# Turning q and k by squares of 32 from the sixteenth pair of heads, and natural token order from the third batch

## The chip, the cores and the metric

The kernel runs on one core of a Trainium2 chip. A core has TensorE (PE in the profile) for matrix products, VectorE (DVE), ScalarE (ACT) and GpSimd (POOL) for elementwise work, and SyncE (SP), whose queue issues nearly all of this kernel's DMA transfers. Each engine has its own list of instructions; semaphores order them against each other. The metric is the time of one execution on the device in microseconds (us); less is better.

## What is computed

Attention with normed queries and keys, then a two-layer network with the activation h - tanh(h):

```python
# q, k, v: (8 batches, 12 heads, 448 tokens, 64); g_q, g_k: (64,)
def rmsnorm(x, g):
    rms = np.sqrt(np.mean(x * x, axis=-1, keepdims=True) + 1e-06)
    return x / rms * g
q_n, k_n = rmsnorm(q, g_q), rmsnorm(k, g_k)
scores = 1.0 / np.sqrt(64) * np.matmul(q_n, k_n.transpose(0, 1, 3, 2))
attn = np.exp(scores - np.max(scores, axis=-1, keepdims=True))
attn = attn / (np.sum(attn, axis=-1, keepdims=True) + 1e-09)
o = np.matmul(attn, v)
x = o.transpose(0, 2, 1, 3).reshape(8 * 448, 12 * 64)
h = x @ w_in                       # w_in: (768, 2048)
out = (h - np.tanh(h)) @ w_out     # w_out: (2048, 768)
```

All data are float32, the weights float64 in memory.

## The kernel before, in words

Heads are taken two at a time, so there are 8 x 6 = 48 pairs, numbered s = 0 to 47; six pairs make a batch. The program is written out by hand, slot by slot: one slot of the schedule per pair (the functions `first_slot`, `early_slot` and `slot`). What stands in a slot for pair s is mixed with preparations for the pairs s + 1 to s + 4. Between these pieces, `run(gap)` draws as many matrix products of the network's stream (`mlp`, a generator) as fit a budget of time; the stream is one batch behind attention. In a slot from 12 on there are eight such runs, and each batch's stream fills six slots: three with the first layer (`hidden`), three with the second (`project`).

*The stream.* Both layers use a scheme of seven products in place of eight (`products`, line 712; the products are the matmuls of L733). A product's weights come from a ring of six slots in SBUF that SP fills from scratch memory (`ring_load`, L386 and L388), five products ahead. Each product is added into s1, s2 or s5 on DVE or ACT as soon as it is done (L787 to L803), and three PSUM banks take turns, with products 2, 3 and 7 accumulating on top of 1, 5 and 6. In the first batch the weights are still being made: each 768 KB piece of float64 words is fetched (`w_raw`, L265 and L269), rounded in three stages on ACT (L71, L72), DVE (L78 to L82) and POOL (L90), with three buffers for the raw words. That ends in slot 10; the first batch's second layer (`project_first`, L898) runs in slots 9 to 11.

*The old way of q and k.* `load` (through `fetch`) brings q and k of pair s + 4 in slot s. `squares` takes their squares on ACT (L123, L124), `norm` sums and scales on DVE and raises to the power -1/2 on POOL (L133 to L135), both for pair s + 3; `norm_q` scales q (L410 on DVE, or L408 on ACT for pairs 9 to 14); and `turn` transposes k and q of pair s + 2 on PE, four transposes each (L421, L425), with evictions from PSUM on ACT (L423, L429). The scale of k is applied later, as the per-partition scale of the exponentials (L512).

*By squares of 32.* From batch `FIRST` on, here 3, `by_blocks(s)` is true. `load_blocks` (L447) fetches q and k of pair s + 3 by eight DMAs in 32 x 32 squares of tokens and dimensions; `square_blocks` (L451, ACT), `norm_blocks` (L458 to L463, DVE and one power on POOL), `scale_blocks` (L470, DVE) and `turn_blocks` (L480 and L484, DVE transposes within the squares, L485 on ACT) follow in the next slot, for pair s + 2. Nothing of it is on PE. It needs the pool `late["blocks"]`, opened when `project_first` has ended.

*Order of tokens.* In the first three batches a partition of the q, k and v tiles holds neighbouring tokens (q four of them, k and v three), so that a piece of memory is 1 KB for q and 768 B for v. Squares of 32 keep tokens in natural order, and from batch 3 on v is fetched in natural order too (`fetch(..., in_order)`), in pieces of 256 B; the last 64 tokens of k and v are always apart (L118). `store` (L828) turns a result back and undoes the permuted order for batches below `FIRST`.

*Attention.* `visit` (for pairs from 13) interleaves the products p x v of pair s (L567, L555) with the scores of pair s + 1 (L506); exponentials are on ACT (L512). The sums of the exponentials are folded on DVE (L537 to L545, L640, L642) and spread (L650 to L663).

Queues are strictly what the program order makes them: SP's list holds, in a slot from 12 on, the ring loads of its runs, the loads of v, and the loads of q and k in their places.

Of the kernel before, what the change touches and what calls it, by code (L numbers as in the profile page):

```python
# [20 lines left out]
NCH = 4  # L21
# [71 lines left out]
def fetch(nc, name, t, pair, in_order=False):  # L93

    S = pair.shape[1]
    P = 128
    KF, KR = S // P, S % P
    if name == "q":
        nc.sync.dma_start(
            out=t.rearrange("p h c d -> p h (c d)"), in_=pair.rearrange("h (p c) d -> p h (c d)", c=NCH)  # L100
        )
        return
    full, rest = pair[:, : KF * P].rearrange("h (p c) d -> h p c d", c=KF), pair[:, KF * P :]
    if name == "v":
        last = t[:, :, KF]
    if in_order:
        for h in range(2):
            nc.sync.dma_start(out=t[:, h, :KF], in_=pair[h, : KF * P].rearrange("(c p) d -> p c d", p=P))
    elif name == "v":
        nc.sync.dma_start(  # L110
            out=t[:, :, :KF].rearrange("p h c d -> p h (c d)"), in_=full.rearrange("h p c d -> p h (c d)")
        )
    else:
        last = t[:, KF]
        for h in range(2):
            nc.sync.dma_start(out=t[:, :KF, h], in_=full[h])
    for r in range(2):
        nc.sync.dma_start(out=last[r * KR : (r + 1) * KR], in_=rest.rearrange("h p d -> p h d"))  # L118
# [19 lines left out]
def bounded_path(tc, ctx, q, k, v, moe_w_in, moe_w_out, out, g_col, ident, ones, half_ones, neg_half, early):  # L138
# [17 lines left out]
    nc = tc.nc  # L156
    B, H, S, D = q.shape
    DFF, DM = moe_w_out.shape
    P = 128
    CP = S // NCH  # L160
    NP = H // 2
# [12 lines left out]
    BL = 32  # L174
    KF, KR = S // P, S % P
# [32 lines left out]
    def load(s, names):  # L208
        b, hp = steps[s]
        for name in names:  # L210
            src = {"q": q, "k": k, "v": v}[name]
            if s == 0 and name != "v":
                t = early[name]
            else:
                shape = [CP, 2, NCH, D] if name == "q" else [P, NCH, 2, D] if name == "k" else [P, 2, NCH, D]
                t = nat.tile(shape, F32, name=f"{name}_nat", bufs=3 if name == "v" else 2)
                fetch(nc, name, t, src[b, 2 * hp : 2 * hp + 2], by_blocks(s))
            loaded[name, s] = t


# [172 lines left out]
    def squares(s):  # L393
        squares_of(nc, early["sq"], early["n"], loaded["q", s], loaded["k", s])
# [36 lines left out]

    FIRST, NJ = 3, S // BL

    def by_blocks(s):
        return has(s) and steps[s][0] >= FIRST

    def load_blocks(s):
        b, hp = steps[s]  # L440
        t = loaded["qk", s] = late["blocks"].tile([P, 2, NJ, BL], F32, name="qk_nat", bufs=2)
        for i, src in enumerate((q, k)):
            for h in range(2):
                rows = src[b, 2 * hp + h].rearrange("(j t) (m d) -> m t j d", t=BL, d=BL)
                for m in range(2):
                    r = (2 * h + m) * BL
                    nc.sync.dma_start(out=t[r : r + BL, i], in_=rows[m])  # L447
# [27 lines left out]
    def turn_blocks(s, i):  # L475

        n = normed[s][:, i].rearrange("p j d -> p (j d)")
        if i == 0:
            qT = qkp.tile([P, S], F32, name="qT")
            nc.vector.transpose(out=qT, in_=n)  # L480
            turned[s] = qT
            return
        kT = qkp.tile([P, S], F32, name="kT")
        nc.vector.transpose(out=kT, in_=n)  # L484
        nc.scalar.mul(kT, kT, g_col)  # L485
        turned[s] = None, kT, turned[s]
        del normed[s]

    def sc_bank():
        return bank_of("sc")  # L490
# [38 lines left out]
    def add(s):  # L529

        if s <= NP + NP // 2:
            sums[s] = []
            return
        t = early["sum"]
        sums[s] = [t]
        p = full(s)
        nc.vector.tensor_tensor(out=t, in0=p[0], in1=p[1], op=ALU.add)  # L537
        nc.vector.tensor_tensor(out=t, in0=t, in1=p[2], op=ALU.add)
# [72 lines left out]
    def totals(s, dn):  # L611

        parts = [t[:, h, n * HS : (n + 1) * HS] for t in sums.get(s, ()) for n in range(2) for h in range(2)]
        parts = [(parts, [ones[:, :BL]] * 2)] if parts else []
        if not sums.pop(s):
            for p in full(s):
                parts.append(
                    ([p[:, h, n * HS : (n + 1) * HS] for n in range(2) for h in range(2)], [ones[:, :BL]] * 2)
                )
            last = probs[s, KF]  # L620
            parts.append(([last[:, h, 0] for _ in range(2) for h in range(2)], [half_ones[:, n] for n in range(2)]))
        for i, (moving, by) in enumerate(parts):
            for n in range(2):
                for h in range(2):
                    r = (2 * n + h) * BL
                    nc.tensor.matmul(
                        dn[r : r + BL, :HS], lhsT=by[n], rhs=moving[2 * n + h],
                        start=(i == 0), stop=(i == len(parts) - 1),
                    )
        rs = whole[s] = sp.tile([P, HS], F32, name="rs")  # L630
        nc.vector.reciprocal(rs, dn[:, :HS])  # L631
# [290 lines left out]
    def run(ns):  # L922

        spent[1] += ns
        while spent[0] + 1.0 < spent[1]:
            took = next(stream, None)
            if took is None:
                return
            spent[0] += took
# [4 lines left out]
    def gap_ns(s):  # L934

        if s < 2 * NP:
            return H_NS / 12 if s % NP < 3 else 4 * S / ENGINE_NS * CD * CF / 12
        return (H_NS + O_NS) / (4 * NP)

    def has(s):  # L940
        return 0 <= s < NS

    def first_slot(s):
# [6 lines left out]
        if s > -3:  # L950
            load(s + 4, "qk")
# [5 lines left out]
        if has(s + 2):  # L957
            load(s + 2, "v")
# [18 lines left out]
    def early_slot(s):  # L977
        gap = gap_ns(s)
        totals(s, sc_bank())
        if has(s + 1):  # L980
            scores(s + 1, 0)
            scores(s + 1, 1)
        if has(s + 2):
            load(s + 2, "v")
        run(gap)
        if has(s + 2):
            turn(s + 2, sc_bank(), sc_bank())
        if has(s + 3):
            squares(s + 3)
        if has(s + 4):  # L990
            load(s + 4, "qk")
        run(gap)
        if has(s + 1):
            scores(s + 1, KF)
        av = [sc_bank() for _ in range(2)]
        last_values(s, av)
        divide(s, values(s, av))
        if has(s + 1):
            scores(s + 1, 2)
        for work, n in ((add, 1), (add_last, 1), (norm, 3), (norm_q, 3)):  # L1000
            run(gap / 2)
            if has(s + n):
                work(s + n)

    def slot(s):

        gap = gap_ns(s)
        av = av_banks
        if has(s + 1):
            scores(s + 1, KF)  # L1010
        if s < FOLDED:
            last_values(s, av)
            totals(s, sc_bank())
            divide(s, values(s, av))
            for c in range(KF):
                scores(s + 1, c)
        else:
            visit(s, av)
        if has(s + 2):
            load(s + 2, "v")  # L1020
        if by_blocks(s + 3):
            load_blocks(s + 3)
        blocks = by_blocks(s + 2)
        run(gap / 2)
        if has(s + 1):
            add(s + 1)
        if blocks:
            square_blocks(s + 2)
        run(gap / 2)
        if blocks:  # L1030
            norm_blocks(s + 2)
        elif has(s + 2):
            turn(s + 2, sc_bank(), sc_bank())
        ahead = has(s + 3) and not by_blocks(s + 3)
        if ahead:
            squares(s + 3)
        if has(s + 4) and not by_blocks(s + 4):
            load(s + 4, "qk")
        run(gap / 2)
        folded = has(s + 1) and s + 1 >= FOLDED  # L1040
        if has(s + 1):
            add_last(s + 1)
        if folded:
            fold(s + 1)
        run(gap / 2)
        if blocks:
            scale_blocks(s + 2)
        if ahead:
            norm(s + 3)
        if folded:  # L1050
            gather(s + 1, 0)
        run(gap / 2)
        if blocks:
            turn_blocks(s + 2, 0)
        if folded:
            gather(s + 1, 1)
        run(gap / 2)
        if blocks:
            turn_blocks(s + 2, 1)
        if ahead:  # L1060
            norm_q(s + 3)
        run(gap / 2)
        if folded:
            spread_sums(s + 1)
        run(gap / 2)
# [358 lines left out]
```

## Time and profile before

| what | value |
|---|---|
| median of 3 runs | 1404.11 us (1401.81 to 1405.44) |
| the profiled execution's own time | 1404.34 us |
| its span, first to last instruction | 1402.5 us |
| PE busy, slots of the early part, 206.8 to 240.5 us | 31.70 of 33.70 us |
| PE busy, slots 13 to 15 (323.1 to 407.0 us) | all of it |
| DMA queue of SP | 355120 packets, 248.00 MB, 64.7% of 16 engines' span |
| weight fetches w_raw, second layer | 16 of 768 KB, 5.4 us to landing |
| fetches of q, whole, in the old way | 17 of 224 KB, 4.8 us to landing |
| fetches of q in squares | 120 of 56 KB, 2.4 us to landing |

The profile is of one execution. Times are counted from the first instruction. A row of the groups names a line of the kernel, the engine, the operation, what it writes and reads, its count, then the busy time in us, the mean of one in ns, and the idle time of the engine just before, with what ended it. The chain of work is followed back from the last instruction to what released each step. PE's matmuls are pipelined, so busy times of short runs overlap.

### The profile page before, as it was taken

To read this page: it belongs to the slowest core of one execution; us is meant where nothing else is said; L and a number is where in the kernel's file an instruction comes from. 1 tells how busy PE (TensorE), PEld (TensorE's weight loads), DVE (VectorE), ACT (ScalarE), POOL (GpSimd) and SP (SyncE) were. 2 spreads that over 40 slices of the span, in tenths; PEclk is the share of its full clock that TensorE was granted. 3 is DMA by queue.
4 is the path that set the end of the run, shared out by engine and by line. 5 is a ranking of instruction groups with operands and counts; after the bars stand their busy time and mean duration, and the time that the engine had idled before them with its cause. 6 is when DMAs were issued, how large, how long until landed. Compare 5 with 4: busy or idle time off the path is not lost.

```text
span 1402.5 us, 29929 instructions
## 1 busy us (share of the span) xinstructions
PE 1367.2 (97%) x11864; PEld 1135.0 (81%) x11864; DVE 939.3 (67%) x1530; ACT 506.6 (36%) x1153; POOL 556.4 (40%) x348
## 2 busy tenths in 40 slices
PE   6999899999999999999999999999999999999997
PEld 2458664478888888888889988988988998899997
DVE  3999888866756688567867668656885678632311
ACT  5866554234422433233332333224333243301100
POOL 4665555223532246225544246422462254411310
PEclk9999999999999999999999999999999999999999
DMA  7769788864556656666666666666666666366563
GB/s 174 178 187 252 241 253 212 223 188 153 172 150 179 175 167 172 173 152 200 173 153 173 188 159 180 181 158 175 168 165 175 164 183 186 109 188 179 191 193 91
DMA packets 355273, 250.01 MB, mean 178 GB/s; under 512 B 266484, under 2 KB 297396, under 8 KB 355124
## 3 DMA queue, kind: packets, MB, share of 16 engines
q1 hardware_dynamic: 355120, 248.00, 64.7%
q8 instruction: 96, 1.57, 0.5%
q14 instruction: 53, 0.43, 0.1%
q10 hardware_dynamic: 4, 0.00, 0.0%
HBM read 214.50 MB, written 33.42 MB: 177 GB/s over the span
## 4 chain that ended last, share of the span: by engine, by line
PE 87%; DVE 5%; DMA 3%; ACT 2%; SPq 2%; issue 1%; POOL 0%; DVEq 0%; ACTq 0%
PE mm L733 64%; PE sc L506 9%; PE sc L567 6%; PE mm L898 4%; PE sc L555 1%; PE sc L605 1%; DMA w_raw<-in_moe_w_out_dram 1%; DMA gT<-in_moe_w_in_dram 1%; DMA q_nat<-in_q_dram 1%; ACT p L512 1%; SPq L118 1%; PE mm L605 1%; DMA w_f<-w_out 0%; DVE rs L631 0%; DVE w_out L82 0%
## 5 line engine op out<-in xcount | busy, mean ns | idle before, releaser
L733 PE MATMUL mm<-xT,w_f 128*128 128x224 f32 x1392 | 278.2, 354 | 2.3 <-DVE s L789 2.3
L733 PEld LDWEIGHTS mm<-xT,w_f 128*128 128x128 f32 x1392 | 261.3, 190 | 15.9 <-issue 10.2
L733 PEld LDWEIGHTS mm<-gT,w_f 128*128 128x128 f32 x1344 | 252.8, 190 | 13.2 <-issue 13.2
L733 PE MATMUL mm<-gT,w_f 128*128 128x224 f32 x1344 | 263.0, 354 | 0.0
L506 PE MATMUL sc<-qT,kT 64*32 64x448 f32 (+1 forms) x3072 | 219.3, 507 | 11.7 <-ACT p_last L512 7.8
L463 POOL TENSOR_TENSOR rr_mine<-rr_mine,neg_half 128x28 f32<-128x28 f32 x30 | 145.1, 4837 | 205.5 <-DVE rr_mine L462 205.5
L733 PE MATMUL mm<-tt,w_f 128*128 128x224 f32 x1044 | 208.9, 353 | 0.0
L733 PEld LDWEIGHTS mm<-tt,w_f 128*128 128x128 f32 x1044 | 196.6, 190 | 4.8 <-issue 4.4
L733 PE MATMUL mm<-tg,w_f 128*128 128x224 f32 x1008 | 197.7, 352 | 0.0
L770 POOL TENSOR_TENSOR gT<-s,th 128x448 f32<-128x448 f32 x96 | 119.1, 1250 | 189.4 <-ACT th L769 184.5
L733 PEld LDWEIGHTS mm<-tg,w_f 128*128 128x128 f32 x1008 | 190.6, 190 | 0.0
L506 PEld LDWEIGHTS sc<-qT,kT 64*32 64x32 f32 x3072 | 75.3, 106 | 87.7 <-issue 52.9
L671 DVE TENSOR_TENSOR xT<-xT,sc 128x448 f32<-128x448 f32 x35 | 21.7, 621 | 175.5 <-ACT xT L670 146.9
L693 POOL TENSOR_TENSOR tt<-xT,tt 128x224 f32<-128x224 f32 x23 | 31.4, 1367 | 243.6 <-DVE xT L675 222.0
L650 ACT COPY sum_g<-sum 32x14 f32<-32x14 f32 x280 | 56.2, 201 | 183.7 <-DVE sum L642 178.0
L567 PE MATMUL sc<-p,v_nat 64*32 64x448 f32 x1120 | 110.5, 536 | 0.0
L769 ACT ACTIVATE th<-s 128x448 f32<-128x448 f32 x96 | 55.2, 575 | 116.4 <-DVE s L795 57.2
L512 ACT ACTIVATE p<-sc 128x448 f32<-128x448 f32 x120 | 65.3, 544 | 58.0 <-PE sc L506 34.5
L135 POOL TENSOR_TENSOR rr<-rr,neg_half 112x8 f32<-112x8 f32 (+1 forms) x36 | 59.6, 1678 | 61.8 <-DVE rr L134 37.8
L898 PE MATMUL mm<-gT,w_out 128*128 128x448 f32 x192 | 75.5, 548 | 0.2 <-POOL w_out L90 0.2
L898 PEld LDWEIGHTS mm<-gT,w_out 128*128 128x128 f32 x192 | 36.1, 192 | 38.5 <-issue 36.4
L567 PEld LDWEIGHTS sc<-p,v_nat 64*32 64x32 f32 x1120 | 42.0, 107 | 30.6 <-issue 30.6
(151 smaller groups left out, 1853.7 us busy)
## 6 DMA issues: line engine op xcount, KB each, us to landing
w_f<-w_in SPq DMA_DIRECT2D x196, 384.0 KB, 3.3
w_f<-w_out SPq DMA_DIRECT2D x147, 512.0 KB, 4.0
w_raw<-in_moe_w_out_dram SPq DMA_DIRECT2D x16, 768.0 KB, 5.4
out_dram<-th SPq DMA_DIRECT2D x192, 56.0 KB, 1.9
w_in<-w_out SPq DMA_DIRECT2D x21, 384.0 KB, 6.5
qk_nat<-in_q_dram SPq DMA_DIRECT2D x120, 56.0 KB, 2.4
qk_nat<-in_k_dram SPq DMA_DIRECT2D x120, 56.0 KB, 2.4
gT<-in_moe_w_in_dram SPq DMA_DIRECT2D x32, 192.0 KB, 4.2
```

The lines of the kernel that those rows point to most:

```text
L135: nc.gpsimd.tensor_tensor(out=r, in0=r, in1=neg_half[:rows], op=ALU.pow)
L463: nc.gpsimd.tensor_tensor(out=mine, in0=mine, in1=neg_half[:, :1].to_broadcast([P, 2 * NJ]), op=ALU.pow)
L506: nc.tensor.matmul(tiles[h][i * BL : (i + 1) * BL, :n], lhsT=kT[r, c * P + at : c * P + at + BL], rhs=qT[r, first : first + n], start=True ...
L512: nc.scalar.activation(p[:, h, c if c < 2 else 0, :], tiles[h][:, :n], AF.Exp, scale=1.0 if rr is None else rr[:, 0, 2 * c + h : 2 * c + h ...
L567: nc.tensor.matmul(av[g][i * BL : (i + 1) * BL, :S], lhsT=v_nat[keys, h, c, m * BL : (m + 1) * BL], rhs=p[keys, h], start=first, stop=True ...
L605: nc.tensor.matmul(av[n][r : r + BL, :HS], lhsT=v_nat[:, h, c, m * BL : (m + 1) * BL], rhs=p[c][:, h, n * HS : (n + 1) * HS], start=False, ...
L650: nc.scalar.copy(out=acc[h * BL : (h + 1) * BL, g], in_=part[g * BL : (g + 1) * BL, h * NJ : (h + 1) * NJ])
L693: eng.tensor_tensor(out=t2, in0=x22, in1=t1, op=ALU.subtract)
L733: nc.tensor.matmul(bank[:, f * HS : (f + 1) * HS], lhsT=w[:, c * width + f, :], rhs=moving[p](c), start=(first and f == 0 and c == 0), sto ...
L769: nc.scalar.activation(th, h, AF.Tanh, bias=0.0, scale=1.0)
L770: eng.tensor_tensor(out=g[:, rows, cols], in0=h, in1=th, op=ALU.subtract)
L898: nc.tensor.matmul(bank[:, :S], lhsT=w_out_row(f, n // HC)[:, n % HC * P : (n % HC + 1) * P], rhs=g[:, f, :], start=(f == 0), stop=(f == C ...
```

## The change

Squares of 32 now begin with pair `TURNED` = 2 x 6 + 3 = 15, in the middle of the third batch (numbered 2), instead of pair 18. Since squares keep the natural order and a batch must have one order, `FIRST` becomes 2: all of the third batch is fetched in natural order. Its first three pairs (12, 13, 14) still go the old way, so `fetch` learns to bring q and k in natural order, in pieces of 256 B: q by two DMAs instead of one. v of pairs 12 to 17 is fetched like that of later batches, by two DMAs for the full part instead of one. The store of the third batch needs no reordering. The fetches of q and k of pairs 15 to 17 in the old way leave slots 11 to 13. The first fetch of squares, of pair 15, stands near the end of slot 12 rather than behind the load of v, since the pool of the squares is opened only within that slot; those of pairs 16 and 17 stand in slots 13 and 14 at the usual place.

```diff
@@ fetch
     if name == "q":
+        if in_order:
+            for h in range(2):
+                nc.sync.dma_start(out=t[:, h], in_=pair[h].rearrange("(c p) d -> p c d", c=NCH))
+            return
         nc.sync.dma_start(
...
     if name == "v":
         last = t[:, :, KF]
+    elif in_order:
+        last = t[:, KF]
     if in_order:
         for h in range(2):
-            nc.sync.dma_start(out=t[:, h, :KF], in_=pair[h, : KF * P].rearrange("(c p) d -> p c d", p=P))
+            to = t[:, h, :KF] if name == "v" else t[:, :KF, h]
+            nc.sync.dma_start(out=to, in_=pair[h, : KF * P].rearrange("(c p) d -> p c d", p=P))
@@ load
-                fetch(nc, name, t, src[b, 2 * hp : 2 * hp + 2], by_blocks(s))
+                fetch(nc, name, t, src[b, 2 * hp : 2 * hp + 2], in_order(s))
@@
-    FIRST, NJ = 3, S // BL
+    FIRST, NJ = 2, S // BL
+    TURNED = 2 * NP + 3
 
     def by_blocks(s):
+        return has(s) and s >= TURNED
+
+    def in_order(s):
         return has(s) and steps[s][0] >= FIRST
@@ early_slot
-        if has(s + 4):
+        if has(s + 4) and not by_blocks(s + 4):
             load(s + 4, "qk")
@@ slot
-        if by_blocks(s + 3):
+        if by_blocks(s + 3) and s + 3 > TURNED:
             load_blocks(s + 3)
...
         if blocks:
             turn_blocks(s + 2, 1)
+        if s + 3 == TURNED:
+            load_blocks(s + 3)
         if ahead:
             norm_q(s + 3)
```

## The prediction

> **What bounds the kernel now.** I read the page's busy row first, then the chain of work that ended last in order of time, then the groups of instructions, the waits, and the timelines of SP, DVE, ACT and POOL around two places. The busy row:
>
> ```profile
> PE 1367.2 (97%) x11864; PEld 1135.0 (81%) x11864; DVE 939.3 (67%) x1530; ACT 506.6 (36%) x1153; POOL 556.4 (40%) x348
> ```
>
> TensorE (PE) is busy 97% of the span: only what shortens PE's own list or opens and closes its gaps counts. The chain in order of time (start, length, what; its longest pieces) splits into slots, one per pair of heads. Slots 13 to 16 and then 19 to 21 read:
>
> ```profile
> 323.11 5.49 PE mm L733 x28
> 329.43 15.91 PE mm L733 x84
> ...
> 351.01 5.49 PE mm L733 x28
> 357.33 15.91 PE mm L733 x84
> ...
> 378.97 5.50 PE mm L733 x28
> 385.29 15.91 PE mm L733 x84
> ...
> 406.98 21.38 PE mm L733 x112
> ...
> 488.03 21.43 PE mm L733 x112
> ...
> 515.13 10.05 PE mm L733 x52
> 525.19 3.40 DMA w_f<-w_out
> 530.14 7.32 PE mm L733 x36
> ...
> 543.05 21.39 PE mm L733 x112
> ...
> 570.05 21.38 PE mm L733 x112
> ```
>
> A slot runs from one first MLP product to the next. Slots 13, 14 and 15 turn q and k on PE: their run of products breaks at 323.11 + 5.49 = 328.60 and resumes at 329.43, 0.83 us later. Slots 19 and 21 turn squares on VectorE (DVE) and have no break. Slot 20 has none, but a hole instead. The waits name it:
>
> ```profile
> PE mm L733 <- DVE s L789: 2.9, 6, 0.6
> ```
>
> In the DVE timeline of slot 20 the sum at L789, which PE needs before product 3, starts at 529.47 and ends at 530.08; PE's previous run (527.27 plus 12 x 0.19) would have let it go on at 529.55. DVE is late because from 522.54 it works without a pause through L458 to L462 (the block norm, 2.2 us), L780 and L781, two L545, L640 and L642, all queued ahead. The "DMA w_f<-w_out" in the chain is only a side branch of that walk. The same hole stands at 856.19, and the chain breaks at the same place in every batch turned by squares (third slot of six).
>
> The third place is early. The weights are still being rounded in slot 10:
>
> ```profile
> 228.30 0.83 SPq L110
> ...
> 232.35 5.67 DMA w_raw<-in_moe_w_out_dram
> 238.04 0.89 ACT w_out L71
> ```
>
> SP works off its list without a pause, so the last weight fetch leaves at 232.35; ScalarE (ACT) waits for it 6.37 us, the exponentials behind it are late, and PE stands 2.03 us before 240.54. From there to 295 PE is full (33.36 of 33.40 us in 240.5 to 273.9), so what is lost there is lost for good.
>
> **What the Trainium skill says.** "TensorE: Matmul & The Clock Gate", architectural detail: ScalarE's and VectorE's queues are strictly first in, first out. The trace agrees: L789 waits 7.5 us behind work that it does not need. The same page, part 1: the array's clock halves for windows of about 3.4 us after idleness. The trace agrees in outline: in 242.3 to 257.5 the granted clock is 0.94, and 32 L898 products take 13.11 us instead of the 12.22 us of the runs at 206.83 and 274.87. "DMA: Bandwidth & Descriptors", specifications: transfers under 512 B per descriptor miss line rate. The trace agrees: its packets take 13 ns on average at 128 B, 18 ns at 256 B, 44 ns at 768 B and 63 ns at 1 KB, 10, 14, 17 and 16 B/ns.
>
> **The change part by part.**
>
> *Pairs 15, 16, 17, on PE.* Out go eight transposes a pair, from these groups:
>
> ```profile
> L425 PE MATMUL sc<-ident,n 112*128 112x112 f32 x72 | 11.2, 283 | 2.4 <-DVE g_col L1381 2.3 <-DVE n L410 0.2
> L421 PE MATMUL sc<-ident,k_nat 128*128 128x128 f32 x40 | 6.1, 274 | 0.4 <-DVE rs L631 0.4
> ```
>
> By busy time 4 x 0.156 + 4 x 0.152 = 1.23 us, but ends overlap; the break of 0.83 us is what they cost on the path. The stages behind carry the rest: attention after a slot takes 351.01 - 345.34 = 5.67, 5.73 and 5.78 us in slots 13 to 15, and 5.59 to 5.70 in 16 to 19.
>
> *The same pairs, other engines.* ACT loses two squares and two evictions (0.654 + 0.637 + 0.631 + 0.546 = 2.47 us), gains L451 and L485 (0.953 + 0.668 = 1.62), and its six full exponentials fall from 0.639 to 0.544. DVE loses 2 x 0.68 (L133), 0.417 + 0.189 (L134) and 1.195 (L410) = 3.16 us and gains L458 1.063, L460 4 x 0.242, L461 0.188, L462 0.179, L470 1.417, L480 0.638, L484 0.627 = 5.08. POOL swaps two powers of 1.68 for one of 4.84. SP swaps five fetches for eight (8 x 0.48 = 3.8 us). All lies beside PE, except where DVE is late. Rather than add these, I take the whole from slots at the same place of their batch, which already do all of it: slots 13 to 15 took 406.98 - 323.11 = 83.87 us, slots 19 to 21 took 570.05 - 488.03 = 82.02 (27.10, 27.92, 27.00). Gain 1.85 us: 0.80 in slot 13, 0.04 in slot 14, 1.01 in slot 15. In slot 14 the removed break comes back as the hole: there L803 starts 6.91 us after the slot's first product, in slot 20 6.87, so DVE is as late.
>
> *What is shifted.* Slot 12 loses pair 15's squares, norm and L410, beside a full PE: nothing. The first fetch of squares (pair 15) stands near slot 12's end. SP's ring loads of that stretch leave at 309.89 and 312.16, so it starts there; eight issues are 3.8 us, landing takes 2.4 (at most 4.5): there by 316 to 321. ACT squares them after slot 13's first products, 323.11 + 2.67 = 325.8. Slack about 5 us; nothing. Two ring loads queue behind those 3.8 us; they run five products of 2.28 us ahead, so nothing. If that cover were gone each us would be one on PE. The fetches dropped from slots 11 to 13 free SP 3.7 us each and a wait of 3.38 us before a k fetch (L116), which nobody waited for: nothing. The third batch's stores read straight (L828 at about 0.62 instead of 0.95 us, six times, 2 us of DVE) in slots where PE waits for no store: nothing.
>
> *Natural order.* q of pairs 12 to 14 becomes two fetches of 256 B pieces instead of one of 1 KB: one more issue (0.4 to 0.5 us of SP; the nearest row, L108, has 0.48), and 896 x 18 ns instead of 224 x 63 ns, over 16 engines 1.0 instead of 0.9 us. k keeps its issues and 256 B pieces. v of pairs 12 to 17 becomes two issues of 0.48 for one of 0.44, and 768 x 18 instead of 256 x 44 ns: 0.9 instead of 0.7 us. In slots 12 on, hidden by the ring's lead. In slot 8 the next weight fetch (163.36) waits for POOL, with 3.7 us of slack on SP: nothing. In slot 9 the next one (205.62) follows back to back, so it slips 0.4, but the round after it waits for POOL and DVE: nothing, at most 0.4. In slot 10 v of pair 12 stands in the chain above: its issue took 1.29 us there, since SP was slowed; two take 0.96 if they run free (0.3 less) and up to 2.4 if both are slowed (1.1 more), plus 0.2 to 0.3 of data ahead of the weight. Bounds -0.1 to +1.4; I take +0.6, about the middle. Whether the half-speed window at 242 to 257 stays is another 0.9 either way.
>
> *Sum.* -1.85 + 0.6 = -1.25 us. The profiled execution took 1404.34 us (span 1402.5), so 1403.1; it lies 0.23 above the median 1404.11, which goes to 1402.9.
>
> **Rivals.**
>
> *A. The hole does not come to slot 14, and the early half-speed window goes.* Then slot 14 gains about 0.95 too and 0.9 comes early: -2.8 - 0.9 + 0.6 = -3.1, about 1401.0. For it: the window depends on a 2 us idleness. Against: the hole is in every like slot, at equal DVE offsets.
>
> *B. Slower: the small-piece fetches hold the weight chain in slots 8 to 10.* Place: SP between two w_raw fetches, with ACT, then PE, behind. It decides once the three slots lose more than 1.85 us together; with 1.5 us each, 4.5 - 1.85 = +2.65, 1406.8. Against: slack of 3.7 us in slot 8 and a POOL wait in slot 9. For: in slot 10 SP's issues already run at up to three times their usual length. Slower by 0.3% would need 6.1 us.
>
> *C. The first fetch of squares is late.* If ACT stands for it at 325.8, tanh and exponentials behind it stand too; two or three us late would cancel the gain: about 1404. Against: the slack of 5 us.
>
> **How the numbers follow.** A change of under 0.3%, 4.2 us, can hardly be told from none here; the three runs themselves span 3.6 us. Forecast (gain of 0 to 2.5 us) 0.60; A 0.17; B 0.13; C 0.05; something not seen 0.05. The low end takes A with a little over a third of the runs' spread (1401.0 - 1.4), the high end B up to near its worked value (1406.4): 1399.6 to 1406.4. Faster by over 0.3% needs A with luck or more: 0.09. Slower by over 0.3% needs a double B: 0.06. The rest 0.85.
>
> **What would show it.** 24 L421 and L425 transposes fewer (12 each), no break in slots 13 and 15, periods of 27.0 to 27.1; slot 14 without break but with PE waiting for L789, period 27.9. Slot 12 as before, 27.9. No ACT wait at L451 for qk_nat. In slots 8 to 10 the w_raw fetches at most 1 us later and PE's stand near 240 between 1.9 and 3.5 us. It would be wrong if slots 13 to 15 summed to more than 83 us, or if PE reached slot 12 over 2 us later than 295.21.

## The result, and the profile after

The changed kernel takes 1401.60 us in the median of 22 runs (1399.12 to 1403.29), the kernel before 1403.95 us in as many (1401.12 to 1405.56). The ratio is 0.9984, with a 95% interval of 0.9977 to 0.9990: 2.3 us less, between 1.4 and 3.2. The forecast was 1.25 us less, 1402.9 us, in a range of 1399.6 to 1406.4. The profiled execution of the changed kernel took 1401.5 us, with a span of 1399.7.

In what follows, a stand is time in which an engine waits, and a fetch lands when its data have arrived. Lines after L98 have moved: by 4 to 7 within `fetch`, by 7 in the functions of the old way behind it and by 11 in the stream and the squares (L733 is now L744, L789 is L800, L421 is L428, L447 is L458, L269 is L276).

The busy row of the page after, to be held against that of before:

```profile
PE 1362.9 (97%) x11840; PEld 1131.4 (81%) x11840; DVE 939.6 (67%) x1545; ACT 502.9 (36%) x1147; POOL 561.7 (40%) x345
```

PE has 24 instructions fewer, the transposes of three pairs. The groups of instructions show it, twelve fewer of each kind (q went from 72 to 60, k in the sc banks from 40 to 28):

```profile
L432 PE MATMUL sc<-ident,n 112*128 112x112 f32 x60 | 8.8, 271 | 2.3 <-DVE g_col L1394 2.1 <-DVE n L417 0.2
L428 PE MATMUL sc<-ident,k_nat 128*128 128x128 f32 x28 | 4.3, 275 | 0.4 <-DVE rs L642 0.4
```

The chain of work in order of time, slots 12 to 16:

```profile
294.27 5.50 PE mm L744 x28
300.59 15.90 PE mm L744 x84
...
322.18 21.40 PE mm L744 x112
...
364.30 7.33 PE mm L744 x36
...
377.27 21.38 PE mm L744 x112
...
404.35 21.38 PE mm L744 x112
```

Slot 12 still breaks for the transposes of pair 14; slots 13 and 15 have no break. Slot 14 has none either, but the chain leaves PE in it, as it did in slot 20 before. The timeline of DVE in slot 14 names the place:

```profile
360.19 1.26 DVE L556 TENSOR_TENSOR rows<-rows,p_last 64x448 f32<-64x448 f32 x2
361.48 1.11 DVE L651 STREAM_TRANSPOSE sum_T<-rows 128x896 f32<-128x896 f32 x1
362.63 1.08 DVE L653 TENSOR_REDUCE sum<-sum_T 128x28 f32<-128x896 f32 x1
363.63 0.61 DVE L800 TENSOR_TENSOR s<-mm,s 128x448 f32<-128x448 f32 x1
```

L800 ends at 364.24, and PE, which waits for it, goes on at 364.30. PE's own timeline has the slot's first products and this wait (the second row ends where that answer's window ended):

```profile
349.15 3.29 PE L744 MATMUL mm<-xT,w_f 128*128 128x224 f32 x16
364.30 1.97 PE L744 MATMUL mm<-xT,w_f 128*128 128x224 f32 x9 [0.51 <-DVE s L800]
```

In that timeline slots 13 to 16 start at 322.11, 349.15, 377.20 and 404.28, so the three slots take 27.04, 28.05 and 27.08 us. By the chain it is 404.35 - 322.18 = 82.17 instead of 83.87, 1.70 us less. The other difference between the two profiled executions lies ahead of these slots: slot 12 starts at 294.27 instead of 295.21. 1.70 + 0.94 = 2.64 of the 2.8 us between the spans. Whether the 0.94 us belong to the change was the first question for the chip.

### The profile page after: what moved, and what is told of

It is laid out like the page before. It is cut to its first block, busy times and chain, and to the rows that moved or that the text cites. A ratio compares the mean times of both kernels' runs of the same rounds, so it can differ in the third digit from the quotient of the medians.

```text
span 1399.7 us, 29908 instructions
## 1 busy us (share of the span) xinstructions
PE 1362.9 (97%) x11840; PEld 1131.4 (81%) x11840; DVE 939.6 (67%) x1545; ACT 502.9 (36%) x1147; POOL 561.7 (40%) x345
## 4 chain that ended last, share of the span: by engine, by line
PE 84%; DVE 8%; DMA 3%; ACT 2%; issue 1%; SPq 1%; POOL 0%; DVEq 0%; ACTq 0%
PE mm L744 62%; PE sc L517 9%; PE sc L578 6%; PE mm L909 4%; PE sc L566 1%; PE sc L616 1%; DMA q_nat<-in_q_dram 1%; PE mm L616 1%; DVE rows L549 1%; DVE rs L642 1%; ACT p L523 1%; DVE w_out L82 1%; DVE rows L556 0%; DMA w_in<-w_out 0%; DVE sum_T L651 0%
## 5 line engine op out<-in xcount | busy, mean ns | idle before, releaser
L744 PE MATMUL mm<-xT,w_f 128*128 128x224 f32 x1392 | 278.5, 354 | 2.8 <-DVE s L800 2.8
L744 PEld LDWEIGHTS mm<-xT,w_f 128*128 128x128 f32 x1392 | 261.3, 190 | 17.1 <-issue 10.2
L744 PEld LDWEIGHTS mm<-gT,w_f 128*128 128x128 f32 x1344 | 252.8, 190 | 13.2 <-issue 13.2
L744 PE MATMUL mm<-gT,w_f 128*128 128x224 f32 x1344 | 263.0, 354 | 0.0
L474 POOL TENSOR_TENSOR rr_mine<-rr_mine,neg_half 128x28 f32<-128x28 f32 x33 | 159.7, 4841 | 220.8 <-DVE rr_mine L473 220.8
L744 PE MATMUL mm<-tt,w_f 128*128 128x224 f32 x1044 | 208.9, 353 | 0.0
L744 PEld LDWEIGHTS mm<-tt,w_f 128*128 128x128 f32 x1044 | 196.6, 190 | 4.9 <-issue 4.4
L744 PE MATMUL mm<-tg,w_f 128*128 128x224 f32 x1008 | 197.5, 352 | 0.0
L744 PEld LDWEIGHTS mm<-tg,w_f 128*128 128x128 f32 x1008 | 190.7, 190 | 0.0
L523 ACT ACTIVATE p<-sc 128x448 f32<-128x448 f32 x132 | 71.9, 544 | 64.0 <-PE sc L517 39.9
L142 POOL TENSOR_TENSOR rr<-rr,neg_half 112x8 f32<-112x8 f32 (+1 forms) x30 | 49.6, 1677 | 38.0 <-DVE rr L141 37.8
```

Of the source, the lines that this page charges most:

```text
L142: nc.gpsimd.tensor_tensor(out=r, in0=r, in1=neg_half[:rows], op=ALU.pow)
L474: nc.gpsimd.tensor_tensor(out=mine, in0=mine, in1=neg_half[:, :1].to_broadcast([P, 2 * NJ]), op=ALU.pow)
L523: nc.scalar.activation(p[:, h, c if c < 2 else 0, :], tiles[h][:, :n], AF.Exp, scale=1.0 if rr is None else rr[:, 0, 2 * c + h : 2 * c + h ...
L744: nc.tensor.matmul(bank[:, f * HS : (f + 1) * HS], lhsT=w[:, c * width + f, :], rhs=moving[p](c), start=(first and f == 0 and c == 0), sto ...
```

## The experiments

All ratios are to the kernel before, run on the same chip.

**1. Natural order alone.**

```diff
-    TURNED = 2 * NP + 3
+    TURNED = 3 * NP
...
-        if by_blocks(s + 3) and s + 3 > TURNED:
+        if by_blocks(s + 3):
...
-        if s + 3 == TURNED:
-            load_blocks(s + 3)
```

> The third batch keeps natural order (fetches of q, k, v and the store), but its pairs are all turned on PE as before. My theory: the 256 B fetches are hidden except in slot 10; slots 13 to 15 keep their breaks (83.9 us for the three), and the time is within 1 us of before, ratio 0.9995 to 1.0005. In the profile PE's first layer of the second batch (slot 12) starts between 294.0 and 296.0 us. Rival B (the small-piece fetches hold the weights): +1.5 us or more, slot 12 starts after 296.5. A rival from the profile after (the weight fetch of slot 8 landed 0.9 us earlier there, 4.7 instead of 5.6 us, because of the smaller pieces ahead of it): -0.9 us, and that landing again at 4.7 us.

Measured: 1403.88 us, ratio 1.0001 (0.9993 to 1.0010). The chain of this kernel keeps its breaks:

```profile
322.43 5.49 PE mm L744 x28
328.74 15.91 PE mm L744 x84
...
406.30 21.38 PE mm L744 x112
```

406.30 - 322.43 = 83.87 us, as before. Slot 12 starts at 294.52. The weight fetch of slot 8 kept ScalarE waiting 5.83 us, between the 6.14 of before and the 5.44 of after; in the later experiments 3, 4 and 7, with the changed kernel's code up to there, it was 5.45, 6.51 and 5.77. By the medians the natural order alone is worth something between 1.0 us less and 1.4 us more: nothing that can be told from zero, and rival B, which needs more than 1.85 us of loss, is out.

**2. Squares alone.**

```diff
-    FIRST, NJ = 2, S // BL
+    FIRST, NJ = 3, S // BL
```

> Pairs 15 to 17 by squares, but fetches of pairs 12 to 14 and of v and the store of the third batch as before; so tokens of pairs 15 to 17 stand in another order than v and the rest of their batch, and the order of the output is not the reference's. My theory: slots 13, 14, 15 take 27.1, 28.0, 27.1 us as in the profile after, 1.7 us less than before; ratio 0.9988 with the early part unchanged (slot 12 starts near 295.2). The rival that the smaller fetches brought the early 0.9 us: then this kernel lacks it and starts slot 12 at 295.2, not at 294.3; if it starts near 294.3 all the same, the early part is scatter between executions.

Measured: 1402.57 us, ratio 0.9987 (0.9978 to 0.9995).

```profile
323.70 21.40 PE mm L744 x112
...
365.83 7.33 PE mm L744 x36
...
378.80 21.39 PE mm L744 x112
...
405.88 21.38 PE mm L744 x112
```

405.88 - 323.70 = 82.18: the whole gain in the slots comes from the squares. Slot 12 starts at 295.80, later than in any other of these kernels, so this one execution alone does not say whether its old fetches are why. Its run of 32 products near 241 took 14.50 us instead of 13.11 before: the array's half-speed window there (a stretch in which the granted clock is 0.50) was 6.8 us long instead of 3.4. Ahead of it this kernel was not late: PE begins the 32 products of slot 9 at 205.88, as in the changed kernel, and the kernel before at 206.83.

**3. The changed kernel once more.**

> The changed kernel once more, for a second profile. If the early gain of 0.94 us belongs to the change, slot 12 starts near 294.3 us again and the weight fetch of slot 8 lands after 4.7 us; if it is scatter, it starts anywhere from 294 to 296. Slots 13 to 15 again 27.1, 28.0 and 27.1 us within 0.1. Ratio 0.9984, as before.

Measured: 1402.45 us, ratio 0.9990 (0.9981 to 0.9998); slots 13 to 15 take 404.94 - 322.77 = 82.17. Slot 12 starts at 294.86: of the 0.94 us, 0.35 are left. Of the five executions so far, the two with the old fetches do start slot 12 later (295.21 and 295.80) than the three in natural order (294.27, 294.52 and 294.86), but for different reasons: the kernel before is late already at slot 9, where squares alone, with the same old fetches, is not, and squares alone loses its time in the longer half-speed window. So the old fetches do not explain the 0.94 us, and experiment 1 has no gain in its median. One traced execution of each kernel can't exclude a smaller part. The three slots give 83.87, 82.17, 83.87, 82.18 and 82.17 and sort by the turning alone.

**4. The fold one run later in the third slots.** The scaling of the squares and the gather behind the fold move back with it.

```diff
-        if folded:
+        third = s % NP == 2 and blocks
+        if folded and not third:
             fold(s + 1)
         run(gap / 2)
-        if blocks:
+        if folded and third:
+            fold(s + 1)
+        if blocks and not third:
             scale_blocks(s + 2)
...
-        if folded:
+        if folded and not third:
             gather(s + 1, 0)
         run(gap / 2)
+        if third:
+            scale_blocks(s + 2)
+            gather(s + 1, 0)
```

> The changed kernel, where in the third slot of each batch (14, 20, 26, 32, 38, 44) the fold of the sums stands one run of products later and the scaling of the squares one run later too, so that DVE reaches the sum of product 5 (L789 before, L800 after) 2.2 us earlier. My theory, that PE's hole in these slots is DVE's queue: the hole goes, each of the six slots takes 27.0 to 27.1 instead of 28.0 us, 5.5 us less in all, ratio to before 0.9945. Rival: the hole is due to the ring's weight fetch that the chain of work names there, or moves to the next product in the same slot: then the slots stay at 28.0 us and the ratio is 0.998.

Measured: 1396.3 us, ratio 0.9951 (0.9937 to 0.9964). DVE in slot 14 of this kernel:

```profile
358.74 1.26 DVE L556 TENSOR_TENSOR rows<-rows,p_last 64x448 f32<-64x448 f32 x2
360.04 0.62 DVE L800 TENSOR_TENSOR s<-mm,s 128x448 f32<-128x448 f32 x1
360.58 1.10 DVE L651 STREAM_TRANSPOSE sum_T<-rows 128x896 f32<-128x896 f32 x1
```

and its chain:

```profile
347.78 21.39 PE mm L744 x112
...
374.80 21.38 PE mm L744 x112
```

L800 now stands ahead of the fold's L651 and L653, and slot 14 takes 27.02 us. The hole was DVE's order of work, not the ring's DMA that the chain names beside it: no DMA was touched. Slots 13 to 15 take 401.88 - 320.73 = 81.15. The two medians of this chip, 1402.45 and 1396.3, differ by 6.2; six slots at 0.99 are 5.9. The chains agree: from the start of slot 13 to the last unbroken run of 112 products it is 1219.82 - 322.18 = 897.64 us in the changed kernel and 1212.49 - 320.73 = 891.76 here, 5.88 less.

**5. Two more issues ahead of the last weight fetch.** The changed kernel and experiments 1 and 3 had shown the fetch of v in two pieces delaying the weight fetch of slot 10, and yet not the weights. So the issue was made longer still. (Lines here are 2 further on.)

```diff
+            src = pair[h, : KF * P].rearrange("(c p) d -> p c d", p=P)
+            for a, z in ((0, 64), (64, 128)) if split else ((0, 128),):
+                nc.sync.dma_start(out=to[a:z], in_=src[a:z])
...
+                ..., in_order(s), name == "v" and s == 2 * NP)
```

> The changed kernel with v of pair 12 (slot 10) fetched by four DMAs instead of two, same bytes and pieces: two more issues, about 1 us of SP, ahead of the last weight fetch. My theory after the first runs: what lands there is bound by the data still ahead in the DMA queues, not by the moment of issue (two issues for one put the fetch 0.7 us later after the one before it, and its landing took 0.7 us less), so from one weight fetch to ScalarE's start on the next stays within 0.4 us of 13.0 us. Rival, the step of my forecast that priced SP's time one for one: it becomes 14.0 us and PE's stand near 240 grows from 2.1 to about 3.1 us.

Measured: 1403.99 us, ratio 0.9998 (0.9988 to 1.0009). SP's queue in slot 10, and ScalarE's wait:

```profile
224.81 0.37 SPq L278 DMA_DIRECT2D w_raw<-in_moe_w_out_dram  x1
...
227.51 3.54 SPq L117 DMA_DIRECT2D v_nat<-in_v_dram  x4
...
233.62 0.46 SPq L278 DMA_DIRECT2D w_raw<-in_moe_w_out_dram  x1
```

```profile
238.60 0.89 ACT L71 ACTIVATE w_out<-w_raw 128x768 f32<-128x768 f32 x1 [7.21 <-DMA w_raw<-in_moe_w_out_dram]
```

From one weight fetch (224.81) to the start on the next weight (238.60) it is 13.79 us: neither within 0.4 of 13.0, as my theory had it, nor 14.0, but near the rival. PE's stand near 240 is 2.86 us, against 2.14 in the changed kernel. The table puts the kernels together; each row is from the timelines of SP and ScalarE in slot 10.

| kernel | fetch to next fetch, us | that fetch to ScalarE's start, us | sum, us |
|---|---|---|---|
| before | 7.28 | 5.69 | 12.97 |
| squares alone (v as before) | 7.24 | 5.85 | 13.09 |
| changed | 8.07 | 5.01 | 13.08 |
| natural order alone | 7.85 | 5.12 | 12.97 |
| changed, again | 7.90 | 4.96 | 12.86 |
| two more issues | 8.81 | 4.98 | 13.79 |

Experiments 4 and 7, with the changed kernel's code here, give sums of 13.18 and 12.85. It looks as if the first 0.6 to 0.8 us of later issue were made up by the landing, and only the next 0.8 us lost. The traces speak for another reading. In the microsecond before that fetch leaves, the DMA engines' share is 0.28 to 0.32 in all six rows, so hardly any earlier transfer still held them; and in the packets of the traces the first of the fetch starts 1.25 to 1.28 us after it leaves in all six, however late that is. SP's time therefore counts one for one. What differs is the end: the last packet is through 4.94 and 5.04 us after the fetch leaves in the two kernels with the old fetches, and after 4.55 to 4.60 in the other four. The fetch of q behind it goes out in those four as two fetches of 256 B pieces, and in the two as one of 1 KB pieces. So the shorter landing goes with what is queued behind, not with being late; but no run changes that fetch of q alone, and its cause is not shown.

**6. v behind the weights.**

```diff
@@ early_slot
-        if has(s + 2):
-            load(s + 2, "v")
         run(gap)
...
+        if has(s + 2):
+            load(s + 2, "v")
         if has(s + 4) and not by_blocks(s + 4):
             load(s + 4, "qk")
```

> The changed kernel with the load of v in slots 6 to 11 moved behind the run of products, beside the loads of q and k, so that in slot 10 v (256 KB, about 4 us of SP as slowed there) is behind the last weight fetch instead of ahead of it. If only the data ahead counts: 256 KB in small pieces are about 1.1 us of the 16 engines, so PE's stand near 240 falls from 2.1 to about 1 us, and with it maybe the half-speed window near 250: 1 to 2 us less than the changed kernel. If SP's time counts one for one: the fetch leaves about 3 us earlier and the stand vanishes, 2.1 us less or more. Rival: v's data now stand ahead of other weights or of q and k in slots 6 to 9, and what is gained in slot 10 is lost there: no difference.

Measured: 1398.85 us, ratio 0.9962 (0.9951 to 0.9974). SP and ScalarE in slot 10:

```profile
225.10 0.37 SPq L276 DMA_DIRECT2D w_raw<-in_moe_w_out_dram  x1
...
229.99 1.19 SPq L276 DMA_DIRECT2D w_raw<-in_moe_w_out_dram  x1
231.28 0.94 SPq L115 DMA_DIRECT2D v_nat<-in_v_dram  x2
```

```profile
235.56 0.97 ACT L71 ACTIVATE w_out<-w_raw 128x768 f32<-128x768 f32 x1 [3.49 <-DMA w_raw<-in_moe_w_out_dram]
```

The changed kernel itself was not run on this chip; by the ratios, 0.9962 against its 0.9984 and 0.9990, this is 3.1 to 3.9 us less. The fetch leaves 4.89 us after the one before it and the sum is 10.46 us, 2.6 less than in the changed kernel: most of SP's time counts here, not only the data, which the expectation put at 1.1 us. PE's stand near 240 is gone, and so is the half-speed window, worth some 1.5 us in the changed kernel (see below): the run of 32 products takes 12.22 us instead of 13.00, and slot 12 starts at 291.20. The rival may have come true in part. PE begins the run of 32 products in slot 9 at 206.85, as in the kernel before (206.83), but at 205.87 to 206.54 in the seven other executions of this document with v at its old place, and at 207.82 in experiment 8, which has v late too. Two executions can't tell that from scatter.

**7. The first fetch of squares, late on purpose.**

```diff
+        if s + 2 == TURNED:
+            load_blocks(s + 2)
         if blocks:
             square_blocks(s + 2)
...
-        if s + 3 == TURNED:
-            load_blocks(s + 3)
```

> The changed kernel with the first fetch of squares (pair 15) moved from the end of slot 12 to slot 13, right ahead of its squaring on ScalarE, for the price of a late fetch (rival C). SP reaches that place about 320 us at the earliest and needs 3.8 us for eight issues and 2.4 to land: ScalarE waits 2 to 4 us for qk_nat in slot 13, with tanh and the copies of the stream behind it. My theory: PE loses up to that much in slot 13 (27.1 becomes 29 to 31 us). Rival: DVE and PE have leeway of 3 us there and nothing is lost.

Measured: 1406.42 us, ratio 1.0016 (1.0009 to 1.0023). The timeline of ScalarE in slot 13,

```profile
328.85 0.95 ACT L462 ACTIVATE qk_n<-qk_nat 128x896 f32<-128x896 f32 x1 [5.32 <-DMA qk_nat<-in_k_dram]
```

and of PE:

```profile
338.22 6.49 PE L744 MATMUL mm<-tt,w_f 128*128 128x224 f32 x24 [1.97 <-DVE s L807]
```

ScalarE stands 5.32 us, longer than the 2 to 4 that I expected, since SP began these eight issues only at 322.60. PE reaches slot 16 at 409.27 and, with 27.90 us for slot 12 from 294.39, slots 13 to 15 take 86.98 us, 4.8 more than in the changed kernel. That is not all the wait itself: the 24 products at 338.22 take 6.49 us where the changed kernel's take 4.72, in a half-speed window (the granted clock is 0.73 from 338.2 to 344.5). So some 3.0 us are stands of PE, and 1.8 the clock behind them. At the end of slot 12, where the change puts this fetch, it leaves at 307.10 to 311.13 and ScalarE takes the data at 323.30 without a wait.

**8. Both improvements.** The edits of 4 and 6 together.

> The changed kernel with the fold one run later in the third slots (as in the run that took 1396.3 us) and v later in slots 6 to 11. The two act in different places, so the gains add: 1394.3 to 1396.0 us, ratio to before 0.993 to 0.9945. If v later brings nothing: 1396.3 us.

Measured: 1393.7 us, ratio 0.9926 (0.9914 to 0.9938), 10 us less than before and the fastest of all, 0.6 under the range that was expected. Slots 13 to 15 take 401.26 - 320.11 = 81.15 as in 4; the run near 241 takes 12.22 us as in 6. Within the noise the gains add.

## Why the prediction was right, and where it was off

*Squares in slots 13 to 15: right.* Forecast 27.10, 27.92 and 27.00 us, measured 27.04, 28.05 and 27.08; gain 1.85 forecast, 1.70 measured, and 1.69 or 1.70 in the five executions with the squares and the fold at its place (the changed kernel and experiments 2, 3, 5 and 6), with the order changed or not. Taking whole slots from the same place of a later batch, rather than adding rows, carried this: by busy time of the transposes alone it would have been 3.7 us.

*The hole that replaces a break: right.* Slot 14 gained nothing. Experiment 4 shows the cause as the forecast named it: DVE reaching product 5's sum late; of the work queued ahead of the sum, it moved the fold. One reading was too large: 7.5 us is how long DVE works without a pause up to that sum in slot 20, but product 5, begun at 522.73 by PE's timeline, was done only near 525.1, so the sum stood about 4.4 us behind other work. Half of rival A, that the hole stays away from slot 14, is out.

*Natural order, +0.6 us: off.* The step priced SP's longer issue in slot 10 one for one and added the data ahead. SP did leave the last weight fetch 0.6 to 0.8 us later, within the bounds given, and one for one agrees with experiment 5. What the step left out is the time from the fetch to ScalarE's start, which became about 0.7 us shorter; data of v ahead of the weight did not show. The sum of issue and landing stayed at 12.85 to 13.18 us, against 12.97 and 13.09 with the old fetch, so in the traces the term is zero within 0.2 us. The medians of experiment 1 alone would allow 0.6 as well. The low bound, -0.1, held it; the value in the middle did not. Without it the forecast is 1402.26 us.

*The half-speed window, 0.9 us either way: right that it matters, priced too low, and not the change's.* The window is not near 250, as an expectation has it: it lies between 239 and 246 us (in the kernel before the granted clock is 0.50 from 240.8 to 243.8), and so takes in the 14 products of the scores ahead of the run of 32. The kernel before, the changed one and experiment 4, in this order:

```profile
240.54 1.74 PE sc L506 x14
242.27 13.11 PE mm L898 x32
```

```profile
239.71 1.74 PE sc L517 x14
241.45 13.00 PE mm L909 x32
```

```profile
239.80 0.98 PE sc L517 x14
240.78 12.22 PE mm L909 x32
```

Both together take 14.85, 14.74 and 13.20 us, and 14.89 in experiment 3: the window costs 1.5 to 1.7 us, where the forecast counted the run of 32 alone. In experiment 4 it is absent, though PE stood 2.25 us just ahead. The page that the forecast cites for it, "TensorE: Matmul & The Clock Gate" of the Trainium skill, part 1, asks for an idle window of about 3.4 us; here stands of 1.93 to 2.17 us went ahead of it. It comes and goes between executions of the same code and adds to the scatter of the medians.

*The total: right, with some luck.* The measured 1401.60 us is nearer to rival A's 1401.0 than to the forecast's 1402.9, but neither half of A is why: the hole came, and the window is in both profiled executions of the changed kernel. The 1.70 us of the slots lie inside the measured interval of 1.4 to 3.2 us less, and on the second chip (experiment 3) the medians differ by 1.7. That the first chip gave 2.3 is within the noise.

*Rival B, the fetches of small pieces hold the weights: out,* by experiment 1. Its mechanism is real: SP's longer issue counts, as experiment 5 shows with 0.7 us. In the changed kernel the shorter landing makes up for it.

*Rival C, the fetch of squares late: out for the change.* In experiment 7 a stand of ScalarE of 5.32 us cost 4.8, of which some 3.0 directly; that such a delay cancels the gain was rightly priced. The slack of about 5 us was in fact larger: the data were asked for by 311.13 and used at 323.30, so with the 2.4 to 4.5 us of landing that the forecast took it was 7 us or more.

*The shifted and dropped work at nothing: right as far as seen.* Slot 12 took 322.18 - 294.27 = 27.91 us, before 27.90.

## What to carry to other kernels

Where the same schedule repeats, forecast an edit from slots at the same place in the cycle that already do it: they contain the next wait as well as the saved one. A removed break gives time back only if the engine that is late next is not late at that very place; there, the order of its queue can be worth more than the edit (here 1.7 us from the edit, 5.9 from six moved folds). Price an issue on a DMA queue from the fetch before it to the use of the data, one for one, and look at what is queued behind the fetch as well as ahead of it: here the landing changed by as much as the issue. And before a difference in the early part is put down to a change, compare the same place in several executions: two late starts can have two reasons.

## What the runs showed of the hardware that was not expected

A weight fetch of 768 KB was used 5.69 and 5.85 us after it left where the fetch of q behind it came as one fetch of 1 KB pieces, and 4.85 to 5.24 us after where q came as two fetches of 256 B pieces, though its first packet started equally soon, within 1.25 to 1.28 us. That the fetch behind is the cause is not shown. Further delay of the issue, by 0.7 to 0.9 us, was not made up (4.98 us).

The half-speed window of the array near 242 us was 3.4 us in six of the ten profiled executions, 6.8 in one, absent in one with a stand of 2.25 us ahead of it, and absent in the two without a stand. Where it came, the stand ahead of it was 1.93 to 2.17 us, in one case 2.86. It costs 1.4 to 1.7 us over the 13.20 us of undisturbed scores and products, and 3.0 when it is 6.8 us long, where the whole change is worth about 1.7.
